# A spectral mixing layer and a two-layer MLP on one core: moving the filter products of four k1 from the vector engine to GpSimd and swapping two blocks in the prologue

## Chip, cores, metric

One core of a Trainium2 chip runs the whole program. The metric is the device time of one execution in microseconds, lower is better; times are medians of several executions, each the span of the core plus some 2 us around it. Ratios are the mean time of one kernel's fast executions over the mean of the other's fast executions of the same rounds, so they are not quite the ratio of the medians quoted beside them.

## The reference

```python
def _attn_ref(x, filt_r, filt_i):             # x: (8, 3008, 256)
    X = np.fft.rfft(x, axis=1)
    F = (filt_r + 1j * filt_i)[None, :, :]
    return np.fft.irfft(X * F, n=x.shape[1], axis=1).astype(np.float32)

def _moe_ref(x, w_in, w_out):                 # 24064 tokens, 256 -> 2048 -> 256
    h = x @ w_in
    return (np.maximum(0.01 * h, h) @ w_out).astype(np.float32)
```

The result is `_moe_ref` of `_attn_ref`, as float32.

## The kernel before

The transform of 3008 = 94 x 32 points is done as small DFTs by matmul. The main loop (47 chunks of 512 tokens of the MLP) carries the transforms of batches 1 to 7 along with it. Batch 0 has nothing to hide behind, so its transform is a prologue, split in two halves of 128 channels (`hf` 0 and 1). For each half and each k1 there is a second forward DFT, two products with the filter (`fa`, `fb`), and an inverse DFT. The products are done either by the vector engine straight from PSUM, or (`on_pool`) by GpSimd, called Pool in the profile, from a copy that ScalarE makes:

```python
def first_s2(hf, c, n, kind, on_pool=False):
    ps = bank(kind, n, DH)                       # "ph": two wide PSUM tiles in turn, "pf": three single ones
    for j in range(n):                           # one 128x128 matmul per k1
        nc.tensor.matmul(ps[:, j, :]..., f2_sb[:, c + j, :], src[:, c + j, ...], ...)
    ...
    if on_pool:
        for j, xf in enumerate(xs):
            act(xf[:], ps[:, ts(j, 4), :])       # ScalarE: PSUM -> SBUF
        for i in range(2):
            for j, xf in enumerate(xs):
                nc.gpsimd.tensor_tensor(y[i][:, ts(j, 4), :], xf[:], fs[i][:, ts(j, 4), :], AL.mult)
    else:
        for i in range(2):
            nc.vector.tensor_tensor(y[i], ps, fs[i], AL.mult)

def first_sa(hf, c, n=4):                        # inverse DFT, two 512-column matmuls per four k1
    for j in range(0, n, 4):
        ps = bank("pf", 4, DH)
        for i, m in enumerate((inv2, inv2x)):
            nc.tensor.matmul(ps, m, y[i][:, ds(j, 4), :], start=(i == 0), stop=(i == 1))
        act(paired(big[2])..., ps...)            # ScalarE empties the bank

# ... the part of the prologue that the change touches
t1_part(0, 3, True)()                            # last transpose of step 1; half 1 can start behind it
upper(1, fa_sb, act)                             # ScalarE copies fa to the upper partitions
first_s2(0, 16, 4, "pf"), first_s2(0, 20, 4, "pf")
upper(1, fb_sb, dve)                             # the vector engine does the same for fb
keep_warm(4)                                     # idle-filling matmuls
first_s2(1, 0, 8, "ph")
first_sa(0, 0, 8)
first_s2(1, 8, 8, "ph", True)
nc.gpsimd.dma_start(w_out_sb[:], ...)
first_sa(0, 16), first_sa(0, 20), first_sa(0, 8, 8)
first_s2(1, 16, 4, "pf"), first_s2(1, 20, 4, "ph")
# ...
```

## Time and profile before

| | before |
|---|---|
| time, median of 3 | 780.8 us (779.73 to 781.11) |
| tensor engine busy | 768.5 us, 99% of the span |
| main loop starts | 39.36 us |
| tensor engine idle ahead of the second half | 20.86 to 22.87 us |
| half clock | 24.33 to 27.74 us |

Pool's timeline (start, length, engine, line, operation, output and inputs, shapes, count, and in brackets the idle time before and who ended it), here its second half and the gap ahead of it:

```profile
23.39 1.11 POOL L136 DMA_DIRECT2D x_sb<-in_x_dram  x2
26.65 2.27 POOL L278 TENSOR_TENSOR prod<-fx_h_c,fa_sb 128x512 f16<-128x512 f32 x2 [2.14 <-ACT fx_h_c L275]
```

and the tensor engine's timeline at the start of the main loop:

```profile
39.36 1.31 PE L377 MATMUL ph<-yt,w_in_sb 128*128 128x512 f16 x4
```

I measure the prologue by one stretch, **R**: from the first matmul behind the tensor engine's gap (22.87) to this line (39.36), so R = 16.49 us. What lies before the gap depends on when loads land and moves by more than half a microsecond from execution to execution; R leaves that out.

### The profile page before, as it was taken

The numbers are of one execution on the slowest core, as the hardware profiler recorded it, in microseconds if no ns is written. First come the engines' busy times: TensorE is split into PE (matmuls) and PEld (weight loads), VectorE is DVE, ScalarE is ACT, GpSimd is POOL, SyncE is SP. The second block draws the span as 40 slices with busy tenths as digits, with TensorE's granted clock in tenths as the row PEclk, the third lists the DMA queues.
The fourth block names the chain that finished last, engine by engine and source line by source line (L and its number), as shares of the span: only waits on it lengthen the run. The fifth ranks groups of instructions, "written<-read, shape, count | busy, mean of one in ns | idle before, by whom it ended". The sixth has DMA issues, their size and how long they took to land.

```text
span 778.8 us, 13329 instructions
## 1 busy us (share of the span) xinstructions
PE 768.5 (99%) x5688; PEld 521.5 (67%) x5688; DVE 369.6 (47%) x468; ACT 553.5 (71%) x784; POOL 148.7 (19%) x123
## 2 busy tenths in 40 slices
PE   8899999999999999999999999999999999999998
PEld 4556666666776676666777667666667667666666
DVE  5989742765238641576407743187523764200000
ACT  5777768676787768777686775967668676666663
POOL 6854200330005200042002410025000330000000
PEclk9999999999999999999999999999999999999999
DMA  9951013210151010510105010230101010110111
GB/s 186 227 92 56 28 41 71 66 42 29 41 108 42 28 41 28 116 35 28 42 28 122 28 41 29 53 96 28 41 28 42 28 38 31 41 42 28 41 41 55
DMA packets 36154, 43.36 MB, mean 56 GB/s; under 512 B 8130, under 2 KB 34370, under 8 KB 35330
## 3 DMA queue, kind: packets, MB, share of 16 engines
q0 software_dynamic: 10208, 17.01, 12.4%
q1 hardware_dynamic: 25888, 25.52, 9.3%
q8 instruction: 44, 0.72, 0.4%
q14 instruction: 14, 0.11, 0.1%
HBM read 34.10 MB, written 24.64 MB: 75 GB/s over the span
## 4 chain that ended last, share of the span: by engine, by line
PE 96%; DVE 2%; ACT 1%; DMA 1%; issue 0%; DVEq 0%; POOLq 0%
PE ph L377 41%; PE po_ps L391 41%; PE pf L173 3%; PE pf L241 2%; PE pf L213 2%; PE pf L229 2%; PE pf L391 1%; DMA x_sb<-in_x_dram 1%; DVE big L195 1%; DVE prod L281 1%; PE pf L288 0%; ACT big L183 0%; PE po_ps L316 0%; PE ph L267 0%; PE ph L254 0%
## 5 line engine op out<-in xcount | busy, mean ns | idle before, releaser
L382 ACT ACTIVATE gt_c<-ph 128x1024 f16<-128x1024 f32 x376 | 384.9, 1024 | 195.5 <-PE ph L377 193.4
L377 PE MATMUL ph<-yt,w_in_sb 128*128 128x512 f16 (+3 forms) x1600 | 386.6, 367 | 0.3
L391 PE MATMUL po_ps<-w_out_sb,gt_c 128*128 128x256 f16 x2944 | 381.5, 273 | 0.5 <-ACT ost_c_t L398 0.5
L391 PEld LDWEIGHTS <-gt_c 128*128 128x128 f16 x3008 | 290.5, 98 | 82.3 <-issue 2.4
L377 PEld LDWEIGHTS <-w_in_sb 128*128 128x128 f16 x1600 | 154.4, 98 | 97.5 <-issue 0.4
L222 POOL TENSOR_TENSOR y_b_g<-p_b_g,p_b_g 128x512 f16<-128x512 f32 x84 | 106.8, 1272 | 225.7 <-DVE p_b_g L220 225.7
L195 DVE STREAM_TRANSPOSE big<-big 128x1024 f32<-128x1024 f32 x32 | 56.0, 1846 | 126.0 <-ACT big L183 125.9
L183 ACT CAST big<-pf 128x512 f16<-128x512 f32 x186 | 106.6, 605 | 1.1 <-PE pf L254 1.1
L244 DVE CAST yt<-pf 128x376 f16<-128x376 f32 x112 | 56.4, 545 | 86.0 <-PE pf L241 86.0
L218 DVE TENSOR_TENSOR p_b_g<-pf,fa_sb 128x512 f32<-128x512 f32 x84 | 58.1, 692 | 38.3 <-PE pf L213 35.3
L398 ACT COPY ost_c_t<-po_ps 128x256 f32<-128x256 f32 x184 | 69.4, 377 | 6.6 <-PE po_ps L391 5.4
L203 DVE STREAM_TRANSPOSE big<-big 128x1024 f32<-128x1024 f32 x28 | 51.1, 1936 | 34.0 <-ACT big L183 34.0
L219 DVE TENSOR_TENSOR p_b_g<-pf,fb_sb 64x512 f32<-64x512 f32 x84 | 58.2, 692 | 1.1
L220 DVE TENSOR_TENSOR p_b_g<-pf,fb_sb 64x512 f32<-64x512 f32 x84 | 57.4, 683 | 1.1
L136 POOL DMA_DIRECT2D x_sb<-in_x_dram x13 | 7.1, 548 | 253.7 <-PE pf L173 252.9
L241 PEld LDWEIGHTS <-big 128*128 128x128 f16 x448 | 25.7, 98 | 13.2
L173 PE MATMUL pf<-x_sb,small_sb 94*128 94x512 f16 x112 | 33.6, 380 | 0.2 <-DVE yt L244 0.2
L213 PE MATMUL pf<-big,f_sb 128*128 128x256 f16 x168 | 32.1, 273 | 0.0
L229 PE MATMUL pf<-y_b_g,small_sb 128*128 128x512 f16 x84 | 31.9, 380 | 0.0
L213 PEld LDWEIGHTS <-f_sb 128*128 128x128 f16 x168 | 16.4, 98 | 19.7
L241 PE MATMUL pf<-i_sb,big 128*128 128x94 f16 x448 | 28.7, 206 | 0.0
L173 PEld LDWEIGHTS <-small_sb 94*128 94x128 f16 x112 | 10.7, 98 | 10.5
(50 smaller groups left out, 166.8 us busy)
## 6 DMA issues: line engine op xcount, KB each, us to landing
out_dram<-ost_c_t SPq DMA_DIRECT2D x92, 256.0 KB, 2.1
x_sb<-in_x_dram POOLq DMA_DIRECT2D x5, 1536.0 KB, 11.1
x_sb<-in_x_dram POOLq DMA_DIRECT2D x2, 768.0 KB, 12.1
x_sb<-in_x_dram POOLq DMA_DIRECT2D x3, 480.0 KB, 7.3
w_in_sb<-in_moe_w_in_dram POOLq DMA_DIRECT2D x1, 1024.0 KB, 13.3
w_out_sb<-in_moe_w_out_dram POOLq DMA_DIRECT2D x1, 1024.0 KB, 11.8
x_sb<-in_x_dram POOLq DMA_DIRECT2D x1, 1024.0 KB, 8.1
fa_sb<-in_filt_r_dram POOLq DMA_DIRECT2D x4, 192.0 KB, 8.5
```

What stands on the lines that cost most here:

```text
L173: nc.tensor.matmul(ps, fwd1[:N1], x_sb[:N1, ds(2 * g, 2), :], start=True, stop=True)
L183: copy(paired(dst)[:, ds(n0, nn), ds(e0, de)], ps.rearrange("p n (e t) -> p n e t", t=2))
L195: nc.vector.transpose(o, a)
L213: nc.tensor.matmul(ps[:, j, :], f2_sb[:, 2 * g + j, :], src[:, 2 * g + j, :], start=True, stop=True)
L218: nc.vector.tensor_tensor(p1[:], ps, fa, AL.mult)
L219: nc.vector.tensor_tensor(p2[0:64], ps[64:P], fb[64:P], AL.mult)
L222: nc.gpsimd.tensor_tensor(y1[:], p1[:], p2[:], AL.add)
L241: nc.tensor.matmul(ps[:, j, :], src[:, dt, n2, :], i1_sb[:, n2, :], start=True, stop=True)
L377: nc.tensor.matmul(ph[:, j, ds(o, ln)], w_in_sb[:, dt, ts(ct, P)], yt[:, dt, ds(lo, ln)], start=(dt == 0), stop=(dt == NDT - 1),)
L382: nc.scalar.activation(gts[ci][:, ds(2 * g, 2), :], ph, AF.Lrelu)
L391: nc.tensor.matmul(po, gts[ci][:, ct, ts(tj, P)], w_out_sb[:, ct, :], start=(ct == 0), stop=(ct == NCT - 1))
L398: nc.scalar.copy(ost[:, tj % 2, :], po)
```

## The change

Intent: the vector engine works without a pause up to 28.6 us of the prologue and Pool has a gap of 2.14 us. So Pool takes k1 16 to 19 of the first half as well, and its block of the second half goes first, so that Pool gets its input sooner.

```diff
     nc.sync.dma_start(i1_sb[:], i1_d.ap())
+    first_s2(0, 16, 4, "pf", True)
     for n0 in (0, N2 // 2):
         x_load(1, n0, N2 // 2)
     t1_part(0, 3, True)()
+    first_s2(0, 20, 4, "pf")
     upper(1, fa_sb, act)
-    first_s2(0, 16, 4, "pf"), first_s2(0, 20, 4, "pf")
     upper(1, fb_sb, dve)
     keep_warm(4)
+    first_s2(1, 8, 8, "ph", True)
     first_s2(1, 0, 8, "ph")
     first_sa(0, 0, 8)
-    first_s2(1, 8, 8, "ph", True)
     nc.gpsimd.dma_start(w_out_sb[:], ...)
-    first_sa(0, 16), first_sa(0, 20), first_sa(0, 8, 8)
+    first_sa(0, 20), first_sa(0, 8, 8), first_sa(0, 16)
```

## The prediction

> **What bounds the kernel now.** I read the page first, then the chain of waits piece by piece, then each engine's timeline from 14 to 40 us, then the busy time in half-microsecond stretches.
>
> The page's head and its busy line:
>
> ```profile
> span 778.8 us, 13329 instructions
> ...
> PE 768.5 (99%) x5688; PEld 521.5 (67%) x5688; DVE 369.6 (47%) x468; ACT 553.5 (71%) x784; POOL 148.7 (19%) x123
> ```
>
> The tensor engine is busy 99% of the span: idle time is 778.8 - 768.5 = 10.3 us in all. The main loop starts with the first matmul of line 377, at 39.36 us; its first four hold on until the last piece of yt is there, and from 39.87 us the chain is PE to PE. The change edits the prologue only (batch 0's transform), so it can only move that start, and everything behind it moves along. What sets that start is in the chain in order of time (start, length, what), the part that the change touches:
>
> ```profile
> 21.64 1.18 DVE big L195
> ...
> 22.87 1.04 PE ph L267 x8
> 23.91 1.18 PE pf L288 x4
> 25.08 0.86 PE ph L267 x8
> 25.95 2.67 PE pf L288 x8
> 28.62 0.45 PE pf L267 x4
> ...
> 29.16 2.48 DVE prod L281 x4
> 31.65 2.29 DVE big L296 x2
> ...
> 33.98 0.69 PE pf L305 x15
> ```
>
> Line 195 is the last transpose of step 1, 267 the second forward DFT (one 128x128 matmul per k1), 281 the products with the filter on the vector engine, 288 the inverse DFT, 296 the transposes after it, 305 the last inverse DFT. Between 22.87 and 29.1 us the chain runs through the **tensor engine**, not through the vector engine that the change relieves. The vector engine's timeline says the same:
>
> ```profile
> 25.21 0.95 DVE L311 COPY fb_sb<-fb_sb 64x3072 f16<-64x3072 f16 x1
> 26.20 1.23 DVE L281 TENSOR_TENSOR prod<-ph,fa_sb 128x1024 f16<-128x1024 f32 x1
> 27.34 1.22 DVE L281 TENSOR_TENSOR prod<-ph,fb_sb 128x1024 f16<-128x1024 f32 x1
> 29.16 0.69 DVE L281 TENSOR_TENSOR prod<-pf,fa_sb 128x512 f16<-128x512 f32 x1 [0.61 <-PE pf L267]
> ```
>
> It has no gap up to 28.56 us, then waits 0.61 us for the tensor engine's next block. So only that much separates the two bounds. And the tensor engine is slow there for a reason of its own, seen in the busy times by half microsecond (columns: stretch, length, busy time and count of PE, PEld, DVE, ACT, POOL, then granted clock, DMA share, GB/s):
>
> ```profile
> 22.00:22.50 0.50, 0.00 (x0) 0.00 (x0) 0.50 (x1) 0.50 (x1) 0.50 (x2) 1.00 1.12 203
> ...
> 24.50:25.00 0.50, 0.50 (x4) 0.22 (x3) 0.50 (x2) 0.47 (x1) 0.01 (x1) 0.50 0.85 172
> ...
> 27.00:27.50 0.50, 0.50 (x3) 0.20 (x2) 0.50 (x2) 0.50 (x2) 0.50 (x1) 0.50 0.90 251
> ```
>
> PE is idle for 2.0 us before 22.87 (it waits for the transpose), and then gets half its clock from 24.33 to 27.74 us, 3.41 us long; cutting the stretches finer gives those two edges.
>
> **What the Trainium skill says.** (1) "TensorE: Matmul & The Clock Gate", section "What's actually happening": the clock falls to one half after an idle window of 3413 ns, and the windows run freely, not tied to the kernel's start. The trace agrees on the length (3.41 us), with one difference: 2.0 us idle of 3.41 was enough. Since the phase is free, I expect the drop in some executions and not in others. (2) Same page, "Wait — 56ns, not 53.3ns?": 427 ns per 512 columns at half clock, 216 at full; four pairs of 512-column matmuls in 2.67 us here fit a mix. The 128-column ones don't care: eight took 0.86 us at full clock (22.87 to 23.73) and 0.89 at half (24.88 to 25.77), 107 ns each[...]. (3) "GPSIMD Engine Reference", 3.1: 4497 ns for 2048 fp32 elements of a two-input operation, so 1.12 us for 512; the trace has 1.12 to 1.15 us. (4) "SBUF — State Buffer", "Who interferes with whom": a vector copy in a two-port mode and a Pool operation shut each other out for the whole instruction. Before, the fb copy at 25.21 fell into a gap of Pool (24.5 to 26.65), so the trace shows nothing for or against; after, it falls on a Pool product.
>
> **The change part by part.**
>
> Vector engine, removed: two products of 128x512 (k1 16 to 19 of the first half), 2 x 0.60 us start to start (22.73 to 23.91) = 1.2 us. The fb copy can start at 22.73 + 1.2 = 23.95 instead of 25.21. The filter has landed by some 23.1 us (issues at 14.52 and 15.68; the two later landings took about 7.3 us, an estimate from the four of fb), so it is not a new wait.
>
> Pool, added: two products, 2 x 1.12 = 2.25 us, from 23.40 to 25.65. The two loads of the next batch, 1.11 us, are pushed back to 25.65-26.76. The second half's products then start at 26.76 instead of 26.65 and end at 31.25 instead of 31.11, since Pool waited 2.14 us for ScalarE's copies before. If the fb copy and Pool's product lock each other, add up to 0.95: 32.2 us.
>
> ScalarE, added: one copy of 128x512, 0.55 us, in its gap from 19.34 to 20.86 (it waited for a filter load). Free. Its copies for Pool's second half move up from 25.98 to some 23.9, as their matmuls go first.
>
> Tensor engine: nothing added or removed. All blocks that lie between 22.87 and k1 16 of the second half stay between them; only their order changes: before 8 small, 4 large, 8 small, 8 large; now 16 small, 12 large (one of which groups changes places). Then the block that the vector engine waits for comes out as follows.
>
> With the clock drop as in the trace: small ones to 22.87 + 16 x 0.107 = 24.59. Large ones at 0.427 until 27.74: 7.4 of them; the other 4.6 at 0.216 take 1.0, so 28.74, against 28.46 before. The change puts 512-column matmuls, which suffer from the half clock, where 128-column ones that don't had been: **+0.28 us**. The vector engine has finished the eight k1 by 27.3 (27.9 with the lock) and waits for 29.44; its 1.2 us are lost in that wait. If the window lies 1 us or more earlier, before and after tie at about 28.0, and the loss is 0.
>
> With no drop: before, the tensor engine would be done early, and the vector engine binds at 28.56, 0.6 us better than the trace. After: the block needs the bank that ScalarE frees after its fourth copy. ScalarE's six copies of 0.56 us begin at 25.15; the fourth ends at 27.4, the block at 27.9, the products start at 28.15. Gain over the same state of before: **-0.4 us**.
>
> After this point all is as before, shifted: products 2.48, transposes 2.29, the last step. Pool's end (31.25 to 32.2) comes before or just at its turn (the tensor engine reaches it at about 31.5 without the drop, 32.6 with it). With drop and no drop about equally likely, and early and late windows too, the mean is 0.5 x (+0.15) + 0.5 x (-0.4) = -0.1 us. Added to the runs before, whose mean is 780.55 and median 780.8: **780.5 us**.
>
> **The rivals.** (a) The vector engine sets the prologue's pace, and 1.2 us less on it come through whole: 779.6. For: it is busy without a gap from 14.8 to 28.6. Against: the 0.61 us wait at 29.16, which caps this at nothing with the drop. (b) Pool becomes the bound: 4 products of the second half ending at 32.2 plus two large matmuls and ScalarE's copy make the third transpose wait; it would need to end past 33 to cost 0.5 us: 781.2. (c) The next batch's load is issued 2.3 to 3.2 us later, and took up to 13.6 us to land: the first half by some 38, needed at 40.5 for line 173; tight, but the second half is needed only four slots of 1.3 us later. If it misses, 1 to 2 us: 782. (d) The order keeps the tensor engine better fed and the drop disappears in most executions: -1.1 against the trace: 779.4. Against: the 2.0 us idle before 22.87, which causes it, is not touched.
>
> **The range and the chances.** The executions before span 779.7 to 781.1, which fits the drop coming and going (a drop costs before 0.6 us). Mechanisms (a) and (d) reach 779.4, (b) and (c) 781.2 to 782. So 779.3 to 781.7. Two per cent are 15.6 us, four tenths of the whole prologue of 39 us; nothing here comes near it: 0.99 for the same, 0.005 on either side.
>
> **What would show it.** Right: the first matmul of line 377 within 1 us of 39.36; the fb copy at 24 to 24.6 us; a wait of the vector engine for line 267 that has grown from 0.61 to 1 to 2 us; Pool without its 2.14 us gap; no wait of line 173 for a load; twelve large matmuls in a row, and, if the clock drops, at 427 ns. Lock: fb copy or a Pool product longer by half a microsecond or more. Wrong: products of k1 16 starting before 28 us in spite of a drop, the main loop starting before 38.3 us, or a Pool release ahead of the last transposes.

## The result

| | before | after |
|---|---|---|
| median of 4 | 780.9 us (779.73 to 781.11) | 780.91 us (780.51 to 781.69) |
| R in the profiled execution | 16.49 us | 16.94 us |
| vector engine's wait for the block of k1 16, half 1 | 0.61 us | 1.96 us |

Ratio 1.0004, 95% interval 0.9987 to 1.0022: no difference. The chain in order of time of the changed kernel:

```profile
22.24 1.18 DVE big L195
...
23.46 1.92 PE ph L267 x16
25.38 4.28 PE pf L288 x12
29.66 0.45 PE pf L267 x4
...
30.20 2.48 DVE prod L281 x4
32.69 2.29 DVE big L296 x2
...
35.02 0.69 PE pf L305 x16
```

Sixteen small matmuls in a row, then twelve large ones, then the block that the vector engine needs. Its start, counted from the end of the gap, has gone from 28.62 - 22.87 = 5.75 us to 29.66 - 23.46 = 6.20 in this chain, which begins a piece where the one before ends; in the tensor engine's timeline, which the table further down uses, from 5.59 to 6.04. The vector engine's timeline:

```profile
24.61 1.25 DVE L311 COPY fb_sb<-fb_sb 64x3072 f16<-64x3072 f16 x1
25.89 1.23 DVE L281 TENSOR_TENSOR prod<-ph,fa_sb 128x1024 f16<-128x1024 f32 x1
27.03 1.22 DVE L281 TENSOR_TENSOR prod<-ph,fb_sb 128x1024 f16<-128x1024 f32 x1
30.20 0.69 DVE L281 TENSOR_TENSOR prod<-pf,fa_sb 128x512 f16<-128x512 f32 x1 [1.96 <-PE pf L267]
```

It is done with its eight k1 earlier, counted from the gap, and waits 1.96 us instead of 0.61. So what was taken from it came back as a wait. Pool's timeline:

```profile
23.89 1.15 POOL L278 TENSOR_TENSOR prod<-fx_h_c,fa_sb 128x512 f16<-128x512 f32 x1
25.01 1.87 POOL L278 TENSOR_TENSOR prod<-fx_h_c,fb_sb 128x512 f16<-128x512 f32 x1
26.82 1.11 POOL L136 DMA_DIRECT2D x_sb<-in_x_dram  x2
27.94 2.29 POOL L278 TENSOR_TENSOR prod<-fx_h_c,fa_sb 128x512 f16<-128x512 f32 x2
```

Its gap is gone; one product takes 1.87 us instead of 1.15, while the vector engine's copy of fb beside it takes 1.25 instead of 0.95. The busy times by stretch (columns as in the prediction; the granted clock is the third figure from the end):

```profile
22.50:23.00 0.50, 0.00 (x0) 0.00 (x0) 0.50 (x1) 0.50 (x1) 0.50 (x2) 1.00 1.08 208
...
27.00:27.50 0.50, 0.50 (x3) 0.21 (x2) 0.50 (x2) 0.32 (x1) 0.50 (x2) 0.50 1.07 390
28.50:29.00 0.50, 0.50 (x2) 0.15 (x1) 0.00 (x0) 0.50 (x1) 0.50 (x1) 0.50 0.56 106
```

The gap of the tensor engine (1.92 us) and the half clock are there as before; cut finer, the drop lies from 25.66 to 29.08 us.

### The profile page after: what moved, and what is told of

It reads as the page before. It is cut to its first block, busy times and chain, and to the rows that moved or that the text cites. A ratio compares the mean times of both kernels' runs of the same rounds, so it can differ in the third digit from the quotient of the medians.

```text
span 779.6 us, 13332 instructions
## 1 busy us (share of the span) xinstructions
PE 769.7 (99%) x5688; PEld 522.0 (67%) x5688; DVE 368.9 (47%) x466; ACT 554.6 (71%) x785; POOL 151.8 (19%) x125
## 4 chain that ended last, share of the span: by engine, by line
PE 95%; DMA 2%; DVE 1%; ACT 1%; issue 0%; DVEq 0%; POOLq 0%
PE ph L378 41%; PE po_ps L392 41%; PE pf L173 3%; PE pf L241 2%; PE pf L213 2%; PE pf L229 2%; DMA f_sb<-fwd_const 1%; PE pf L392 1%; DMA x_sb<-in_x_dram 1%; DVE prod L281 1%; PE pf L288 1%; ACT big L183 0%; PE ph L267 0%; DVE big L195 0%; DVE big L296 0%
```

## The experiments

There were nine runs (eight new kernels, and the changed one once more), of five timed executions each. All gave correct results. All ratios are within 0.2% of 1, so the traces, one execution of each, carry most of the argument. The **theory**: in this stretch the tensor engine is the bound because its clock is halved; the change leaves its work and the gap that brings the drop alone, and so returns the vector engine's 1.2 us as a wait. **Rivals**: the new order costs by itself (ScalarE frees the banks too late), or Pool with its added work binds.

One number sorts executions without a trace: the mean granted clock of the whole execution. In seven profiled executions with 0.998 or 0.997 the traces show the drop in the prologue; in four with 0.999 or 1.000 they show none. The last digit also moves with a drop behind the last matmul, where nothing waits for the tensor engine.

### e1: the kernel before with the gap filled

```diff
-    keep_warm(4)
+    keep_warm(12)
```

> The kernel before with eight more idle-filling matmuls ahead of the last transpose of step 1, so that the tensor engine's gap of 2.0 us there shrinks to some 0.3 us. Measure R: from the first matmul behind that gap (second forward DFT, second half) to the first matmul of the main loop; before 39.36 - 22.87 = 16.49 us. My theory (the tensor engine at half clock sets this stretch): no clock drop at all (mean granted clock 1.000 instead of 0.998), the vector engine's wait of 0.61 us gone, R = 15.9, time 0.6 us lower. Rival, the vector engine sets the pace anyway: the same gain of at most 0.6 here, so this run alone doesn't tell them apart, it needs the next. Rival, the drop doesn't come from the gap: clock stays 0.998 and R 16.5.

Measured: 779.87 us against 780.62 (ratio 0.9992, interval 0.9978 to 1.0006); R = 38.83 - 22.97 = 15.86; gap 0.54 us; clock 1.00 through the whole prologue. The tensor engine behind the gap:

```profile
22.97 1.04 PE L267 MATMUL ph<-big,f_sb 128*128 128x128 f16 x8 [0.54 <-DVE big L195]
```

The vector engine's timeline has no wait ahead of this line any more:

```profile
28.64 0.69 DVE L281 TENSOR_TENSOR prod<-pf,fa_sb 128x512 f16<-128x512 f32 x1
```

As the theory said, to the tenth: filling the gap took the drop away, and with it 0.63 us of R. The interval of the times alone would not show it; R does.

### e2: the changed kernel with the gap filled

The same edit on the changed kernel.

> The changed kernel with the same eight more idle-filling matmuls. R after the change was 40.40 - 23.46 = 16.94 us. My theory: with no clock drop the wait of the vector engine falls from 1.96 us to some 0.5 us (what is left is the bank that ScalarE frees), R = 15.5, so 0.4 us shorter than the kernel before with the same filling, and 1.4 us shorter than without it; time 1.4 us lower. Rival, the new order itself costs the time (bank waits of ScalarE's copies): R falls by less than 0.5, to 16.4 or more. Rival, Pool (its second half ends late): R falls by less than 0.7 and the third transpose waits for ScalarE.

Measured: 779.25 us against 780.62 (ratio 0.9985, interval 0.9973 to 0.9998); all five executions at clock 1.000; R = 38.04 - 22.59 = 15.45. The tensor engine, the vector engine and again the tensor engine:

```profile
24.33 2.91 PE L288 MATMUL pf<-prod,small_sb 128*128 128x512 f16 x12
...
31.76 0.38 PE L288 MATMUL pf<-prod,small_sb 128*128 128x512 f16 x1 [0.36 <-POOL prod L278]
```

```profile
27.84 0.69 DVE L281 TENSOR_TENSOR prod<-pf,fa_sb 128x512 f16<-128x512 f32 x1 [0.34 <-PE pf L267]
```

The twelve large matmuls take 2.91 us instead of 4.46. R is 1.49 us shorter than in the first profile of the changed kernel (0.46 shorter than in its second, e9) and 0.41 shorter than in e1. So the change is worth 0.4 us once the drop is gone, and the order by itself doesn't cost what was lost. Pool's end now shows as a first wait of 0.36 us.

### e3: only Pool's added block

```diff
+    first_s2(0, 16, 4, "pf", True)      # and the order 20, 8, 16 of the first half's inverse groups
...
     first_s2(1, 0, 8, "ph")
     first_sa(0, 0, 8)
     first_s2(1, 8, 8, "ph", True)       # as before
```

> Only the first part of the change: Pool takes k1 16 to 19 of the first half too, the order of the second half's blocks stays as before. My theory: the tensor engine's order between the gap and k1 16 of the second half is the old one, so R stays 16.5 (within 0.2, by where the clock drop falls), and the 1.2 us taken from the vector engine come back as wait: 0.6 + 1.2 = 1.8 us. Rival, Pool's extra work costs the time: R 16.8 or more here. Time within 0.3 us of before.

Measured: 780.48 us against 780.62 (ratio 1.0000, interval 0.9987 to 1.0012); R = 39.43 - 22.62 = 16.81, which is 0.1 above the stated range and at the rival's mark. The vector engine:

```profile
29.23 0.69 DVE L281 TENSOR_TENSOR prod<-pf,fa_sb 128x512 f16<-128x512 f32 x1 [1.72 <-PE pf L267]
```

The wait is 1.72 us for 1.8 forecast: the vector engine's saving comes back as a wait with this part alone. But R missed. The drop lay 0.92 to 4.33 us behind the gap here. Half of the time that it spends over large matmuls (1.26 us) puts the block at 5.59 us, and it came at 28.52 - 22.62 = 5.90. The chain of this trace shows where the 0.3 us arose, in ScalarE:

```profile
27.46 0.52 ACT big L289
...
28.03 0.60 PE pf L288 x2
```

ScalarE's copy frees a bank at 27.98 us; only then the last two large matmuls start, at 28.03, and the block comes behind them. Pool doesn't bind: the vector engine waits for the tensor engine, and all transposes behind it run without a pause. ScalarE was late for the most part because the tensor engine was: its copies for Pool, which come just before, began 3.77 us behind the gap (3.11 before), and the second block of eight small matmuls, which they read, at 2.54 (2.01 before), since the drop lay over nearly all of the four large ones ahead of it. That ScalarE would have been as late in the kernel before with the drop at the same place is argued, not shown.

### e4: only the order

```diff
+    first_s2(1, 8, 8, "ph", True)
     first_s2(1, 0, 8, "ph")
     first_sa(0, 0, 8)
-    first_s2(1, 8, 8, "ph", True)
```

> Only the second part: Pool's block of the second half ahead of the vector engine's, products as before. My theory: sixteen small matmuls come first and all twelve large ones in or behind the clock drop: R 16.8 to 16.95, the whole of the 0.45 us by which R grew with the change; the vector engine's wait grows from 0.6 to about 1.0 us. Rival (Pool's extra work is what costs): R stays 16.5. Time 0.3 to 0.4 us above before.

Measured: 780.43 us against 780.62 (ratio 1.0002, interval 0.9989 to 1.0014); R = 39.19 - 22.68 = 16.51. A miss: I had said 16.8 to 16.95, and the rival said 16.5 (the wait, forecast at about 1.0 us, is 0.22). The tensor engine and the vector engine:

```profile
24.42 3.96 PE L288 MATMUL pf<-prod,small_sb 128*128 128x512 f16 x12
```

```profile
28.99 0.69 DVE L281 TENSOR_TENSOR prod<-pf,fa_sb 128x512 f16<-128x512 f32 x1 [0.22 <-PE pf L267]
```

Here the twelve took 3.96 us instead of 4.46: the drop came from 0.80 to 4.21 us behind the gap, so 0.9 us of it fell on small matmuls, which don't feel it. In the profile of the changed kernel it came from 2.20 to 5.62, over large ones only. **So the place of the drop, which differs from execution to execution, moves R as much as either order does**, and single profiles of before and after can't be compared without it. This broke my reading of the result, where I had charged all 0.45 us to the order.

### e9: the changed kernel again, executions sorted by clock

No edit.

> The changed kernel unaltered, beside the kernel before on the same chip, to sort executions of both by mean granted clock: 0.998 or less (the drop in the prologue came) and 0.999 or 1.000 (it didn't). In the last call the kernel before took 780.62 to 780.72 us with it and 779.83 to 780.14 without. My theory: without the drop the changed kernel is 0.4 us below the kernel before without it (779.6), with the drop it is 0 to 0.3 us above (780.6 to 781), so that the medians tie. Rival (the reordering is neutral by itself): no difference in either class. Rival (the changed kernel always has the drop, as in its four executions so far): no execution at 0.999 or above.

Measured: 780.21 us against 780.60 (ratio 0.9998, interval 0.9986 to 1.0011). Five of five executions had the drop, as had the four before: never once was it missing. The kernel before, over the 27 executions that have a clock recorded:

| before | executions | mean | from, to |
|---|---|---|---|
| clock 0.998 or less | 15 | 780.70 us | 780.56 to 781.01 |
| clock 0.999 or more | 12 | 779.85 us | 779.60 to 780.25 |

The two classes of the kernel before don't overlap. The sign isn't perfect for other kernels: the one execution of e4 with a clock of 1.000 took 780.43 us, no less than its others. With the drop, the two kernels tie: the changed one's nine average 780.60 us, the 15 of the kernel before 780.70. They were run at other times. The changed kernel, with the drop each time, spreads from 779.86 to 781.69 us: it has no good class, but a good place for the drop. The profiled execution (779.91 us) shows it; the tensor engine, then the vector engine:

```profile
22.89 1.92 PE L267 MATMUL ph<-big,f_sb 128*128 128x128 f16 x16 [2.25 <-DVE big L195]
24.64 3.37 PE L288 MATMUL pf<-prod,small_sb 128*128 128x512 f16 x12
```

```profile
28.60 0.69 DVE L281 TENSOR_TENSOR prod<-pf,fa_sb 128x512 f16<-128x512 f32 x1 [1.05 <-PE pf L267]
```

The clock where the drop begins, with no matmul running:

```profile
22.30:22.35 0.05, 0.00 (x0) 0.00 (x0) 0.05 (x1) 0.05 (x1) 0.05 (x1) 0.79 0.41 82
```

The drop lay from 22.33 to 25.74 here: it began in the gap, ran through the sixteen small matmuls for nothing, and hit the large ones for 1.1 us. R = 38.80 - 22.89 = 15.91, a microsecond below the first profile of the same kernel. The rival that had the drop in every execution is right; my class of changed executions without it doesn't exist in nine.

### e10: four large matmuls between the small ones

```diff
     first_s2(1, 8, 8, "ph", True)
-    first_s2(1, 0, 8, "ph")
     first_sa(0, 0, 8)
+    first_s2(1, 0, 8, "ph")
```

> The changed kernel with the first four large matmuls put back between the two blocks of eight small ones (8 small, 4 large, 8 small, 8 large, as before; Pool's block still first). The clock drop came in 9 of 9 executions of the changed kernel (mean clock 0.998 or less) but only in 10 of 18 of the kernel before, and in 4 of 5 of the order-only variant. If sixteen small matmuls in a row behind the gap[...] are what keeps the activity low and so brings the drop more often, it is missing here in about two of five executions, and those lie at about 779.4 to 779.7 us, 0.4 below the kernel before without the drop; with the drop 780.0 to 780.9. Rival (the Pool part or chance brings it): it comes in all five. Five executions can only hint at it.

Measured: 779.80 us against 780.56 (ratio 0.9995, interval 0.9981 to 1.0009). Two of five executions had no drop, at 779.15 and 779.35 us; those with it took 779.80, 780.32 and 780.66 (I had said 779.4 to 779.7 without it and 780.0 to 780.9 with it). The two lie 0.6 us below the kernel before without the drop (779.84 on average): so a gain without a drop is seen with the unfilled gap too, in this order. On the number of drops the run is only a hint: the drop came in 18 of 19 executions of the kernels that have sixteen small matmuls in a row and the unfilled gap (after 9, e4 4 of 5, e7 5), and in 22 of 37 with eight first (before 15 of 27, e3 4 of 5, e10 3 of 5); but the idea came from the earlier of these counts, and e10 ran on another chip. The profiles speak against it in part: in e9 and e7 the drop began inside the gap, before any small matmul, and in e4 0.80 us behind it, before the second eight, which alone set the orders apart. Of the four profiled drops only that of the changed kernel's first profile (2.20 us behind the gap) can have come from the sixteen. What brings the drop so often there is open.

### e7: the awaited block moved ahead

On the changed kernel, drop untouched:

```diff
     first_sa(0, 0, 8)
+    first_s2(1, 16, 8, "ph")
...
-    first_s2(1, 16, 4, "pf"), first_s2(1, 20, 4, "ph")
```

> The changed kernel, with the forward DFT of k1 16 to 23 of the second half as one block of eight into a wide bank, right behind the first two inverse groups, so ahead of eight of the large matmuls that the clock drop makes slow. Drop not touched. My theory (the 1.2 us are lost because the vector engine waits for this block): its wait goes, though the clock still drops; the transposes start about 7.2 us behind the end of the gap instead of 9.1, held then by the large matmuls and ScalarE's copies; Pool's end holds the third transpose; R 15.6 to 16.0 against 16.94, time 0.6 to 1.2 us below before. Rival (Pool's end is what binds): R 16.5 or more. Rival (bank waits come instead): vector engine's wait stays above 1 us.

Measured: 779.84 us against 780.60 (ratio 0.9993, interval 0.9979 to 1.0007), with the drop in five of five. The vector engine:

```profile
27.35 1.22 DVE L281 TENSOR_TENSOR prod<-ph,fa_sb 128x1024 f16<-128x1024 f32 x1
...
32.83 2.37 DVE L296 STREAM_TRANSPOSE big<-big 128x1024 f32<-128x1024 f32 x2 [0.85 <-ACT big L289]
```

The wait for the block is gone, and a wait of the third transpose for ScalarE has come in its place. Pool, which I had expected behind it, is not in the chain of this trace; what releases the transpose are four copies of ScalarE in a row, behind the large matmuls:

```profile
30.68 2.12 ACT big L289 x4
```

R = 37.81 - 22.54 = 15.27, below the 15.6 to 16.0 that I gave; 0.1 of it is only apparent, since the main loop's next three matmuls wait 0.22 us more there. The drop lay early, as in e9, whose R was 15.91: with the drop nearly in the same place, moving the block was worth about 0.5 us.

### e5: e7 with the gap filled

The edit of e1 on e7.

> The last one with the gap filled by eight more idle-filling matmuls, so no clock drop. My theory: the vector engine's last wait (0.34 us in the filled changed kernel) goes, but there the third transpose already waited 0.2 us for Pool's end, so Pool and ScalarE bind next: R 15.2 to 15.45, time 0 to 0.3 us below the filled changed kernel, 1.3 to 1.6 below before. Rival (the vector engine still binds): R 15.1 or less, the full 0.4.

Measured: 779.32 us against 780.60 (ratio 0.9986, interval 0.9974 to 0.9999); R = 38.26 - 23.17 = 15.09. The tensor engine, then the vector engine:

```profile
32.14 0.38 PE L288 MATMUL pf<-prod,small_sb 128*128 128x512 f16 x1 [0.42 <-POOL prod L278]
```

```profile
33.19 2.37 DVE L296 STREAM_TRANSPOSE big<-big 128x1024 f32<-128x1024 f32 x2 [0.78 <-ACT big L289]
```

R met the rival's mark (15.1 or less) rather than mine, but the trace shows the waits of the theory: last inverse matmul for Pool, third transpose for ScalarE behind it. In time it is no better than e2 (779.25). It was run at another time. Pool binds now: the chain of this trace runs along Pool up to that matmul.

### e6: e5 with Pool relieved

```diff
-    for n0 in (0, N2 // 2):
-        x_load(1, n0, N2 // 2)
+    x_load(1, 0, N2 // 2)
...
+    x_load(1, N2 // 2, N2 // 2)          # behind Pool's products of the second half
     nc.gpsimd.dma_start(w_out_sb[:], ...)
```

> The last one, with the second half of the next batch's load issued behind Pool's products of the second half instead of ahead of them, so that Pool ends 0.55 us sooner. If Pool's end binds there: R falls by 0.3 to 0.55 against the last one, to some 14.9, time about 1.7 us below before. If not: R as in the last one. The load lands some 3.5 us later, by about 41 to 43 us; it is needed five microseconds into the main loop, at about 43 to 44: if it misses, line 173 waits and the gain is lost.

Measured: **779.08 us** against 780.60 (ratio 0.9983, interval 0.9971 to 0.9996); R = 37.46 - 22.58 = 14.88. The third transpose waits 0.35 us instead of 0.78:

```profile
32.37 2.37 DVE L296 STREAM_TRANSPOSE big<-big 128x1024 f32<-128x1024 f32 x2 [0.35 <-ACT big L289]
```

R fell by 0.21 us, less than the 0.3 to 0.55 expected; the chain now runs through the tensor engine and ScalarE, no longer through Pool. No wait for the load appears in the main loop. This version beats the kernel before by 0.17% and the changed one by 0.15% (e9). What each step gives depends on the order of the steps: filling the gap took 0.63 us off R in the kernel before (e1), and 0.18 once the block had been moved (e7 to e5).

### All profiles in one table

Times in us behind the end of the gap; "block" is the first matmul of k1 16, half 1, in the tensor engine's timeline. R of e7 has the reservation told above. In e10 the vector engine waits 1.21 us earlier, ahead of its eight k1, and not at the block.

| profile | order | drop from, to | block | vector engine's wait | R |
|---|---|---|---|---|---|
| before | 8 small, 4 large, 8, 8 large | 1.46, 4.87 | 5.59 | 0.61 | 16.49 |
| after | 16 small, 12 large | 2.20, 5.62 | 6.04 | 1.96 | 16.94 |
| after (e9) | same | -0.56, 2.85 | 5.00 | 1.05 | 15.91 |
| e3 | as before | 0.92, 4.33 | 5.90 | 1.72 | 16.81 |
| e4 | as after | 0.80, 4.21 | 5.61 | 0.22 | 16.51 |
| e10 | 8, 4 large, 8, 8 large | -0.39, 3.02 | 5.25 | 0 | 16.16 |
| e1 | as before | none | 4.96 | 0 | 15.86 |
| e2 | as after | none | 4.54 | 0.34 | 15.45 |
| e7 | 16, 4 large, block | -0.34, 3.08 | 3.25 | 0 | 15.27 |
| e5 | same | none | 2.62 | 0 | 15.09 |
| e6 | same | none | 2.62 | 0 | 14.88 |

One sum reproduces the block's place in both orders: 16 small of 0.109 and 12 large of 0.216 make 4.33, plus half of the time that the drop spends over large matmuls. Before: 1.26, so 5.59 (measured 5.59). After: 1.70, so 6.03 (6.04). e4: 1.24, so 5.57 (5.61). e9: 0.55, so 4.88 (5.00). e10: 0.87, so 5.20 (5.25). It gives too little by 0.2 to 0.6 where ScalarE has to free the bank first (e1, e2, e3). With it, as an estimate, the kernel before with the drop where the first profile of the changed one had it would have its block at 5.84: the order is worth 0.20 of the 0.45 us there, the place of the drop the rest. The same estimate for the old order gives 5.57 with the drop of e4, a tie, and 5.20 with that of e9, so that the new order gains 0.3 us there.

## Why the prediction was right, and where it wasn't

- **The bound.** Right. The tensor engine set this stretch, through its half clock: e1 and e2 took the drop away and R fell by 0.63 and 1.49 us (0.46 against e9). The rival in which the vector engine sets the pace (779.6 us) falls with e3, where 1.2 us less work became 1.1 us more wait.
- **Large matmuls in the drop, +0.28 us.** The mechanism was right and the size nearly so: by the sum above, an estimate, the new order costs 0.31 us with the drop where the prediction had it, and 0.20 where the changed kernel's first profile has it. No run has both orders with the drop at one place. "Early window: before and after tie" comes out of the sum for e4's place (5.57 us in both orders), but for a still earlier one the new order gains 0.3 us (e9), which the prediction left out.
- **Without a drop, -0.4 us.** Right with the gap filled in both (R 15.45 against 15.86), but it never came about in the changed kernel itself. The products start 27.84 - 22.59 = 5.25 us behind the gap in e2; the prediction's sum has 28.15 - 22.87 = 5.28.
- **"Drop and no drop about equally likely."** This step failed for the changed kernel. It holds for the kernel before (15 of 27 with it). In the changed kernel the drop came in 9 of 9, so the half that should have gained 0.4 us didn't exist. In return the drop cost less than I had it in executions where it fell on the small matmuls (e9, 779.91 us). The two errors nearly cancel, which is luck: the nine executions of the changed kernel average 780.60 us, the mixture of the kernel before 780.3. Nor does the number tell the theories apart: of the rivals, only the missed load (782) lies outside the range of 779.3 to 781.7. That the drop is missing in "most executions" thanks to the order (the fourth rival) is the reverse of what was seen.
- **What a drop costs the kernel before, 0.6 us.** R says 0.63 (e1 against before); the classes of its own executions differ by 0.85.
- **Lock of copy and product.** It took place: copy 1.25 us instead of 0.95, Pool's product 1.87 instead of 1.15, in e3 as well (copy 1.35), and in e4, where the copy fell on a product of the second half (1.36). The forecast was up to 0.95; Pool lost 0.72. It fell beside the path: Pool's end was no wait in the changed kernel, and became one only with the gap filled (e2, 0.36 us; e5, 0.42).
- **The signs.** Wait grown to 1 to 2 us: 1.96. Pool without its gap: yes. No wait for the next batch's load: none. Main loop within 1 us of 39.36: 40.40, just missed, of which 0.59 lies before the gap's end and isn't the change's doing: in e9 the same kernel's gap ends at 22.89, as before. fb copy at 24 to 24.6: 24.61.

Open: why the clock drops in nearly every execution of the kernels with sixteen small matmuls in a row and less often in the others, and whether ScalarE's bank would have cost e3's 0.3 us in the kernel before with the same place of the drop.

## What to carry to other kernels

Before you move work off an engine, look at what it waits for at the end of the stretch: an engine that already waits there for another (0.6 us here) returns nothing when work is taken from it, as long as that wait lasts, and here the bound was a tensor engine at half clock. Where a gap of the tensor engine is followed by a stretch at half clock, fill the gap first (eight idle matmuls took 0.6 us off R before, and 0.5 or 1.5 us after, by the place of the drop), and only then look for what the reordering is worth. When a kernel has two populations of executions, sort them by clock before comparing medians, and don't compare single profiles whose drop lies in different places.

## What the Trainium skill lacked or had wrong

- "TensorE: Matmul & The Clock Gate", section "What's actually happening", has the drop come after at least one idle window. Here no window was idle as a whole: in the changed kernel's first profile the window ahead of the drop (22.25 to 25.66 us, if windows of 3.41 us lie end to end) had 1.21 us of idle time, then small matmuls, and the clock was halved for 3.41 us. No page gives the share of activity that is enough. That the windows run freely agrees: the drop began 0.56 us before the gap's end in one execution of the changed kernel and 2.20 us after it in another.
- The same page, "Back-to-back issue gap", gives some 81 ns per matmul for weight load and matmul pairs of 128 columns and 131 ns for 512 columns. Here eight 128-column pairs took 0.86 us (107 ns each) at full clock and 0.89 us at half, and 512-column pairs 216 ns each at full clock.
- No page says outright that 128-column matmuls, each with its own weight load, don't feel the half clock, so that their order against large ones decides what a drop costs: 0.55 us of added time when sixteen of them and part of the gap lay in it (e9), 1.70 when none did (both are half of the drop's time over large matmuls).
